# Three result buffers for a float64 decode, and scatters of token places through four disjoint views, in a fused attention and two-MoE kernel

## The chip, the cores and the metric

The kernel runs on one core of one Trainium2 chip. The metric is the device time of one execution in microseconds (us). The engines are named as in the profile: PE (TensorE's matmuls) and PEld (its weight loads), DVE (VectorE), ACT (ScalarE), POOL (GpSimd) and SP (SyncE, which here only issues DMAs). SP and POOL each send their DMAs in the order of their program: an issue that waits holds up what stands behind it.

## The reference, cut to what matters

```python
attn = linear_attention(r, k, v, w, u)             # 4 x 8 heads x 768 x 48
x = attn.transpose(0, 2, 1, 3).reshape(3072, 384)  # tokens
# first MoE: one expert of 8 for each token, d_ff 1024
expert = argmax(x @ w_gate, axis=1)
x[mask_e] = gate_w * (relu(x[mask_e] @ w1[e]) @ w2[e])
# second: one dense layer for all tokens, d_ff 2048, weights in float64
h = x @ w_in
out = ((h - tanh(h)) @ w_out).astype(float32)
```

The weights `w_in` and `w_out` come as float64 and have to be turned into float32 on the chip. A token's gated attention output goes to `xd` in DRAM, and the first MoE gathers from there the tokens of one expert at a time.

## The kernel before, in words

The program has three parts, one after the other: attention and gating (to about 184 us), the first MoE (to 415 us) and the second (to 827 us). Every fp32 matrix is split into a high and a low part (`fp32r`) and each product is made in three passes, so ACT casts the high part and DVE or POOL subtracts it from the original to get the low part.

*The first MoE* runs over 8 experts of 8 steps of 128 hidden columns: 64 steps `i`, in program order on every engine. A step issues `mm1(i+2)` (hidden layer of the step after the next: 9 matmuls into `hps`, L986; ACT's ReLU L989; DVE's low part `h`, L990), then `mm2(i)` (9 matmuls into `y`, L1011). In three steps of each expert `xg_trans` turns the next expert's gathered tokens: PE transposes into `tps` (L973), ACT casts (L974), DVE subtracts (`xt`, L975). `tps` and `hps` share four PSUM buffers.

*The weights* come by `w_load` (L76, SP) into four staging buffers `stg`, and `refill` calls `w_split` on them: ACT's cast (L84) and the subtraction (L85), one part in four by DVE and three by POOL. A staging buffer is free when its two parts are split.

*The float64 decode* fills DVE's spare time. 32 pieces of 128 x 384 numbers of the second MoE's weights are loaded by SP as 64-bit integers (`d64`, three buffers), decoded by five DVE instructions (L936 to L943) and stored by SP into `wdec` in DRAM (L951, `dec_move`), from where the second MoE's weights are loaded later. `b` lies in PSUM, `a` in one SBUF buffer, the result `f` in one of two buffers (tag `dcf`, the pool's default). `dec_move` of a step stores what the step before decoded and then issues the next piece's load. In SP's program it stands behind the step's `w_load`s.

*The places of the tokens.* For the output the kernel needs, for each place in the experts' order, the token that lies there. 24 indirect DMAs on POOL's queue (L1178), one about every two steps, scatter 128 token numbers each (`tok`) to their places (`pos`) in `permd` in DRAM; one DMA reads the whole back (`perm`, L1182) in step 54, and DVE turns it into output rows (L1186 to L1193). The places are a permutation, so no two scatters write the same element. They are written as DMAs to one tensor, and each waits until the one before it has landed.

*The overflow path* (`beyond`, L1067 to L1122) handles tokens above an expert's capacity, behind a branch on their number; it uses `permd`, the gather pool and the decode pool. In the profiled execution none of its instructions runs.

Of the kernel before, what the change touches and what calls it, by code (L numbers as in the profile page):

```python
# [8 lines left out]
F32 = mybir.dt.float32  # L9
F32R = mybir.dt.float32r  # L10
F16 = mybir.dt.float16
I32 = mybir.dt.int32
# [8 lines left out]
MIN_EXP = 2.0 ** -15 * 1.125  # L21
# [9 lines left out]
def rwkv_moe_moe_kernel(ctx: ExitStack, tc: tile.TileContext, rk_t, rkv, pk, u, wp1, wp2, out):  # L31


    nc = tc.nc
    B, C, P, _, H, D = rkv.shape
    N, DM = out.shape
# [875 lines left out]
    dcp = m1.enter_context(tc.tile_pool(name="dcp", bufs=2))  # L912
    dc, decoded = {}, []


    UNW = 384
    NU = 1536 // UNW
# [9 lines left out]
    def decode(i):  # L927

        p, q = divmod(i, NU)
        hl = dc.pop(i).bitcast(I32).rearrange("p (n t) -> p n t", t=2)  # L930
        lo, hi = hl[:, :, 0], hl[:, :, 1]

        b = psm.tile([P, UNW], I32, tag="dec", name="dec", bufs=1)
        a = dcp.tile([P, DM], I32, tag="dca", name="dca", bufs=1)[:, 0:UNW]
        f = dcp.tile([P, UNW], F32, tag="dcf", name="dcf")
        nc.vector.tensor_scalar(out=b, in0=hi, scalar1=0x07FFFFFF, scalar2=3,  # L936
                                op0=ALU.bitwise_and, op1=ALU.logical_shift_left)
        nc.vector.scalar_tensor_tensor(out=b, in0=lo, scalar=29, in1=b,
                                       op0=ALU.logical_shift_right, op1=ALU.bitwise_or)
        nc.vector.scalar_tensor_tensor(out=a, in0=hi, scalar=-0x40000000, in1=b,  # L940
                                       op0=ALU.bitwise_and, op1=ALU.bitwise_or)
        nc.vector.tensor_single_scalar(out=b, in_=hi, scalar=0x7FFFFFFF, op=ALU.bitwise_and)
        nc.vector.scalar_tensor_tensor(out=f, in0=b.bitcast(F32), scalar=MIN_EXP, in1=a.bitcast(F32),  # L943
                                       op0=ALU.is_ge, op1=ALU.mult)
        decoded.append((i, f))

# [120 lines left out]
    def beyond(q):  # L1067
# [23 lines left out]
        fetch(tk, permd, pl)  # L1091
        x = xgp.tile([P, DM], F32, tag="xg", name="ov_x")
        fetch(x, xd, tk)
        xT = dcp.tile([P, DM], F32, tag="dca", name="ov_xT", bufs=1)
        ps = psm.tile([P, CAP], F32, tag="h", name="ov_ps", bufs=4)
        for kk in range(KD):
            nc.tensor.transpose(ps[:, kk * P:(kk + 1) * P], x[:, kk * P:(kk + 1) * P], ident)
# [3 lines left out]
        for f in range(CH1):  # L1101
            if f % 2 == 0:
                wa, wb = (dcp.tile([P, DM], U64, tag="d64", name="ov_w", bufs=DB).bitcast(F32) for _ in range(2))
                fetch(wa, halves, ovr[:, f:f + 1])
                fetch(wb, halves, ovr[:, f + 1:f + 2])
            hps = psm.tile([P, CAP], F32, tag="h", name="ov_hp", bufs=4)
            for kk in range(KD):
                c0 = kk * 256 + f % 2 * P
                nc.tensor.matmul(hps[:, 0:P], lhsT=wa[:, c0:c0 + P], rhs=xT[:, kk * P:(kk + 1) * P],
                                 start=(kk == 0), stop=(kk == KD - 1))  # L1110
            h = dcp.tile([P, UNW], F32, tag="dcf", name="ov_h")
            nc.scalar.activation(out=h[:, 0:P], in_=hps[:, 0:P], func=ACTF.Relu)
            for d in range(KD):
                c0 = f % 2 * DM + d * P
                nc.tensor.matmul(yo[d][:, 0:P], lhsT=wb[:, c0:c0 + P], rhs=h[:, 0:P],
                                 start=(f == 0), stop=(f == CH1 - 1))
# [28 lines left out]
    with tc.manual_schedule():  # L1145
# [7 lines left out]
        for i in range(NC1):  # L1153
# [22 lines left out]
            for t in range(*((max(k, 0) * NT // S0) for k in (i - CH1, i - CH1 + 1))):  # L1176
                if t < NT:
                    nc.gpsimd.indirect_dma_start(  # L1178
                        out=permd, out_offset=bass.IndirectOffsetOnAxis(ap=pos[:, t:t + 1], axis=0),
                        in_=tok[:, t:t + 1], in_offset=None)  # L1180
            if i == CH1 + S0 + 2:
                nc.gpsimd.dma_start(out=perm, in_=permd.rearrange("(i p) o -> p (i o)", p=P))  # L1182
# [218 lines left out]
```

## Time and profile before

| what | value |
|---|---|
| timed runs | 825.07, 825.17, 829.99 us, median 825.17 |
| the profiled execution | 828.9 us, span 826.8 us |
| mean granted TensorE clock | 0.987 |
| PE, PEld busy | 786.1 us (95%), 702.3 us (85%) |
| DVE, ACT, POOL busy | 649.6 us (79%), 526.5 us (64%), 448.3 us (54%) |
| DMA | 89.88 MB, mean 109 GB/s |

The span is the time between the first and the last instruction in the trace, and 2.1 us of the execution lie around it. Shares of busy time are means over three parts with different limits, so the rows further below go by stretches. Idle time of an engine is put down to what ended it (`x <- y` reads: x waited for y). In the names, `hps`, `y`, `h` and `xt` are as above; `dcf` is the decode's result, `stg` a staging buffer, `ring` a buffer of split weights. DVEq, SPq and the like are an engine's sequencer or its DMA queue.

### The profile page before, as it was taken

Reading aid. Unit: us, or ns where it says so; the run is one execution under the profiler, and the core shown is the slowest. Engines: PE = TensorE matmul, PEld = TensorE weight load, DVE = VectorE, ACT = ScalarE, POOL = GpSimd, SP = SyncE. Lnnn points to the kernel's source line nnn. Section 1 sums busy time; section 2 is a strip of 40 time slices with the busy share of each in tenths; the row PEclk is TensorE's granted clock in tenths of the full one; section 3 lists DMA queues with packets and bytes.
Section 4 is the critical chain, followed back from the end, with each engine's and each line's share of the span. In section 5 each row is a group of like instructions: output and inputs, shape, how many; then the busy total and the mean of one; then the engine's idle time right before and its main releaser. Section 6 shows DMA issues by size and latency. Waiting matters only on the chain.

```text
span 826.8 us, 14401 instructions
## 1 busy us (share of the span) xinstructions
PE 786.1 (95%) x5052; PEld 702.3 (85%) x5052; DVE 649.6 (79%) x1127; ACT 526.5 (64%) x1135; POOL 448.3 (54%) x438
## 2 busy tenths in 40 slices
PE   7799999989999999997999999999999999999995
PEld 6576766789888999996989999999999999999895
DVE  6789888548888888876469888888888888888991
ACT  7778887515454444443478776776777677677870
POOL 5977876226675886656525535335344344443533
PEclk9799999999999999999999999999999999999999
DMA  8988774226688989897410000000000000000000
GB/s 202 246 222 238 220 211 129 99 71 201 201 227 236 256 224 267 258 250 177 110 56 2 1 1 39 1 1 39 1 1 29 10 1 17 23 1 0 39 1 38
DMA packets 34979, 89.88 MB, mean 109 GB/s; under 512 B 5690, under 2 KB 13022, under 8 KB 34896
## 3 DMA queue, kind: packets, MB, share of 16 engines
q1 hardware_dynamic: 30704, 78.87, 34.5%
q0 software_dynamic: 4192, 9.99, 3.9%
q8 instruction: 42, 0.69, 0.4%
q14 instruction: 41, 0.34, 0.2%
HBM read 73.10 MB, written 15.74 MB: 107 GB/s over the span
## 4 chain that ended last, share of the span: by engine, by line
PE 48%; DVE 2%; issue 1%; POOL 1%; ACT 0%; POOLq 0%; DVEq 0%; ACTq 0%
PE h L1237 23%; PE o L1285 22%; PE y L1011 2%; PE hps L986 1%; DVE t L1258 0%; DVE h L1255 0%; DVE h L1256 0%; DVE h L1254 0%; DVE t L1253 0%; POOL out_dram L1298 0%; POOL g L1274 0%; ACT g L1273 0%; POOLq L1396 0%; ACT z L1241 0%; ACT t L1243 0%
## 5 line engine op out<-in xcount | busy, mean ns | idle before, releaser
L1237 PE MATMUL h<-xb,ring 128*128 128x512 f32 x864 | 215.9, 395 | 0.7 <-DVE t L1258 0.7
L1274 POOL TENSOR_TENSOR g<-t,g 128x512 fp32r<-128x512 f32 x93 | 120.5, 1295 | 176.3 <-ACT g L1273 121.3
L1285 PE MATMUL o<-ring,g 128*128 128x384 f32 x1116 | 209.3, 336 | 0.0
L1285 PEld LDWEIGHTS o<-ring,g 128*128 128x128 f32 x1116 | 196.1, 188 | 8.1
L1237 PEld LDWEIGHTS h<-xb,ring 128*128 128x128 f32 x864 | 161.3, 188 | 31.9 <-DVE t L1258 1.1
L85 POOL TENSOR_TENSOR ring<-stg,ring 128x384 fp32r<-128x384 f32 x102 | 104.9, 1057 | 39.6 <-ACT ring L84 23.9
L1241 ACT ACTIVATE z<-h 128x512 f32<-128x512 f32 x96 | 57.5, 599 | 97.9 <-PE h L1237 97.8
L1011 PE MATMUL y<-h,ring 128*128 128x256 f32 (+7 forms) x576 | 115.5, 345 | 0.0
L986 PE MATMUL hps<-xt,ring 128*128 128x472 f32 (+6 forms) x504 | 106.8, 355 | 8.4 <-DVE xt L975 4.1
L1011 PEld LDWEIGHTS y<-h,ring 128*128 128x128 f32 x576 | 102.6, 190 | 3.5 <-DVE h L990 0.4
L986 PEld LDWEIGHTS hps<-xt,ring 128*128 128x128 f32 x504 | 90.7, 188 | 13.7 <-DVE xt L975 5.5
L1253 DVE TENSOR_TENSOR t<-t,h 128x512 f32<-128x512 f32 x96 | 65.8, 686 | 43.0 <-ACT t L1243 42.9
L84 ACT CAST ring<-stg 128x384 fp32r<-128x384 f32 x152 | 71.1, 511 | 29.3 <-DMA stg<-in_wp_dram 24.9
L1258 DVE COPY_PREDICATED t<-mk,h 128x512 f32<-128x512 uint32 x96 | 72.2, 752 | 9.9
L1255 DVE SCALAR_TENSOR_TENSOR h<-s,h 128x512 f32<-128x512 f32 x96 | 66.9, 696 | 10.0
L1245 ACT ACTIVATE s<-z,gb 128x512 f32<-128x512 f32 x96 | 69.6, 725 | 0.0
L1256 DVE SCALAR_TENSOR_TENSOR h<-z,h 128x512 f32<-128x512 f32 x96 | 66.8, 695 | 3.3
L1247 ACT ACTIVATE mk<-z,gt 128x512 f32<-128x512 f32 x96 | 69.3, 722 | 0.0
L989 ACT ACTIVATE h<-hps 128x256 fp32r<-128x256 f32 (+7 forms) x64 | 32.0, 501 | 57.7 <-PE hps L986 55.3
L1254 DVE TENSOR_TENSOR h<-h,z 128x512 f32<-128x512 f32 x96 | 66.5, 693 | 0.0
L344 ACT ACTIVATE am<-ident,dt 128x128 f32<-128x128 f32 x192 | 58.6, 389 | 7.0 <-DVE dt L337 6.9
L1273 ACT CAST g<-t 128x512 fp32r<-128x512 f32 x93 | 57.6, 619 | 8.0 <-DVE t L1258 5.8
(233 smaller groups left out, 1116.2 us busy)
## 6 DMA issues: line engine op xcount, KB each, us to landing
stg<-in_wp_dram SPq DMA_DIRECT2D x64, 384.0 KB
n<-in_rkv_dram SPq DMA_DIRECT2D x24, 576.0 KB
d<-in_wp_dram SPq DMA_DIRECT2D x32, 384.0 KB
t<-in_rk_t_dram SPq DMA_DIRECT2D x48, 192.0 KB
wdec<-dcf SPq DMA_DIRECT2D x32, 192.0 KB
xd<-xs SPq DMA_DIRECT2D x24, 192.0 KB
stg<-wdec SPq DMA_DIRECT2D x12, 384.0 KB
wl<-wdec SPq DMA_DIRECT2D x2, 768.0 KB
```

The source lines that it names most:

```text
L84: nc.scalar.copy(out=dst[:, 0, sl], in_=of)
L85: eng.tensor_tensor(out=dst[:, 1, sl], in0=of, in1=dst[:, 0, sl].bitcast(F32), op=ALU.subtract)
L986: nc.tensor.matmul(ps, lhsT=wf(a, kk), rhs=xt[e][b][:, kk, :], start=(n == 0), stop=(n == 8))
L1011: nc.tensor.matmul(yps[d], lhsT=wf(a)[:, d * P:(d + 1) * P], rhs=h2[:, b, :], start=(f == 0 and n == 0), stop=(f == CH1 - 1 and n == 2))
L1237: nc.tensor.matmul(ps, lhsT=wf(a, kk), rhs=xb[j][:, b, kk, :], start=(n == 0), stop=(n == 8))
L1245: nc.scalar.activation(out=s, in_=z, func=ACTF.Square, scale=G_K ** 0.5, bias=gb)
L1247: nc.scalar.activation(out=mk, in_=z, func=ACTF.Relu, scale=-1.0, bias=gt2)
L1255: nc.vector.scalar_tensor_tensor(out=ps, in0=s, scalar=G_K * G_D, in1=ps, op0=ALU.add, op1=ALU.mult)
L1256: nc.vector.scalar_tensor_tensor(out=ps, in0=z, scalar=G_A, in1=ps, op0=ALU.subtract, op1=ALU.mult)
L1258: nc.vector.copy_predicated(out=t, mask=mk.bitcast(U32), data=ps)
L1274: nc.gpsimd.tensor_tensor(out=g[:, 1, :], in0=ww, in1=g[:, 0, :].bitcast(F32), op=ALU.subtract)
L1285: nc.tensor.matmul(ops[q], lhsT=gg[i][:, b, q * P:(q + 1) * P], rhs=wf(a), start=(f == 0 and n == 0), stop=(f == CH2 - 1 and n == 2))
```

## The change

The result `f` has three buffers, and the decode's intermediate `a` is the same memory as `f`, read as integers: the third instruction (L940, now L942) writes it and the fifth (L943, now L945) multiplies it in place. The buffer of `a` goes; the overflow path, which used its tag for `xT`, takes a gather buffer. `permd` is seen through four views that the program takes for disjoint; scatter `t` goes through view `t % 4`. Line numbers behind L914 rise by two.

```diff
--- before.py
+++ after.py
@@ -912,6 +912,8 @@
     dcp = m1.enter_context(tc.tile_pool(name="dcp", bufs=2))
     dc, decoded = {}, []
 
+    permv = dram_disjoint_views(permd, 4)
+
 
     UNW = 384
     NU = 1536 // UNW
@@ -931,8 +933,8 @@
         lo, hi = hl[:, :, 0], hl[:, :, 1]
 
         b = psm.tile([P, UNW], I32, tag="dec", name="dec", bufs=1)
-        a = dcp.tile([P, DM], I32, tag="dca", name="dca", bufs=1)[:, 0:UNW]
-        f = dcp.tile([P, UNW], F32, tag="dcf", name="dcf")
+        f = dcp.tile([P, UNW], F32, tag="dcf", name="dcf", bufs=3)
+        a = f.bitcast(I32)
         nc.vector.tensor_scalar(out=b, in0=hi, scalar1=0x07FFFFFF, scalar2=3,
                                 op0=ALU.bitwise_and, op1=ALU.logical_shift_left)
         nc.vector.scalar_tensor_tensor(out=b, in0=lo, scalar=29, in1=b,
@@ -940,7 +942,7 @@
         nc.vector.scalar_tensor_tensor(out=a, in0=hi, scalar=-0x40000000, in1=b,
                                        op0=ALU.bitwise_and, op1=ALU.bitwise_or)
         nc.vector.tensor_single_scalar(out=b, in_=hi, scalar=0x7FFFFFFF, op=ALU.bitwise_and)
-        nc.vector.scalar_tensor_tensor(out=f, in0=b.bitcast(F32), scalar=MIN_EXP, in1=a.bitcast(F32),
+        nc.vector.scalar_tensor_tensor(out=f, in0=b.bitcast(F32), scalar=MIN_EXP, in1=f,
                                        op0=ALU.is_ge, op1=ALU.mult)
         decoded.append((i, f))
 
@@ -1091,7 +1093,7 @@
         fetch(tk, permd, pl)
         x = xgp.tile([P, DM], F32, tag="xg", name="ov_x")
         fetch(x, xd, tk)
-        xT = dcp.tile([P, DM], F32, tag="dca", name="ov_xT", bufs=1)
+        xT = xgp.tile([P, DM], F32, tag="xg", name="ov_xT")
         ps = psm.tile([P, CAP], F32, tag="h", name="ov_ps", bufs=4)
         for kk in range(KD):
             nc.tensor.transpose(ps[:, kk * P:(kk + 1) * P], x[:, kk * P:(kk + 1) * P], ident)
@@ -1108,7 +1110,7 @@
                 c0 = kk * 256 + f % 2 * P
                 nc.tensor.matmul(hps[:, 0:P], lhsT=wa[:, c0:c0 + P], rhs=xT[:, kk * P:(kk + 1) * P],
                                  start=(kk == 0), stop=(kk == KD - 1))
-            h = dcp.tile([P, UNW], F32, tag="dcf", name="ov_h")
+            h = dcp.tile([P, UNW], F32, tag="dcf", name="ov_h", bufs=3)
             nc.scalar.activation(out=h[:, 0:P], in_=hps[:, 0:P], func=ACTF.Relu)
             for d in range(KD):
                 c0 = f % 2 * DM + d * P
@@ -1176,7 +1178,7 @@
             for t in range(*((max(k, 0) * NT // S0) for k in (i - CH1, i - CH1 + 1))):
                 if t < NT:
                     nc.gpsimd.indirect_dma_start(
-                        out=permd, out_offset=bass.IndirectOffsetOnAxis(ap=pos[:, t:t + 1], axis=0),
+                        out=permv[t % 4], out_offset=bass.IndirectOffsetOnAxis(ap=pos[:, t:t + 1], axis=0),
                         in_=tok[:, t:t + 1], in_offset=None)
             if i == CH1 + S0 + 2:
                 nc.gpsimd.dma_start(out=perm, in_=permd.rearrange("(i p) o -> p (i o)", p=P))
```

All engines issue the same instructions in the same order as before; what they wait for differs. The first place is DVE at two decodes in the first MoE, around 240 to 247 us of the trace, before and after. `dec`, `dca` and `dcf` are `b`, `a` and `f`; in brackets are the semaphores that a row waits for, DMAHW ones for SP's transfers.

```order
L940 SCALAR_TENSOR_TENSOR dca<-d_4769,dec 128x384 [waits DVE_49]
L942 TENSOR_SCALAR dec<-d_4769 128x384 [waits DVE_49]
L943 SCALAR_TENSOR_TENSOR dcf<-dec,dca 128x384 [waits DMAHW3_49,DVE_49]
L85 TENSOR_TENSOR ring_4168<-stg,ring_4168 128x384 [waits DMAHW2_49,Activation_49]
L990 SCALAR_TENSOR_TENSOR h_4935<-hps,h_4935 128x440 [waits Activation_49]
L936 TENSOR_SCALAR dec<-d_4820 128x384 [waits DMAHW4_49,DVE_49]
L938 SCALAR_TENSOR_TENSOR dec<-d_4820,dec 128x384 [waits DVE_49]
L940 SCALAR_TENSOR_TENSOR dca<-d_4820,dec 128x384 [waits DVE_49]
L942 TENSOR_SCALAR dec<-d_4820 128x384 [waits DVE_49]
L943 SCALAR_TENSOR_TENSOR dcf<-dec,dca 128x384 [waits DMAHW6_49,DVE_49]
```

The same place in the changed program:

```order
L942 SCALAR_TENSOR_TENSOR dcf<-d_4768,dec 128x384 [waits DMAHW0_49,DVE_49]
L944 TENSOR_SCALAR dec<-d_4768 128x384 [waits DVE_49]
L945 SCALAR_TENSOR_TENSOR dcf<-dec,dcf 128x384 [waits DVE_49]
L85 TENSOR_TENSOR ring_4168<-stg,ring_4168 128x384 [waits DMAHW2_49,Activation_49]
L992 SCALAR_TENSOR_TENSOR h_4931<-hps,h_4931 128x440 [waits Activation_49]
L938 TENSOR_SCALAR dec<-d_4818 128x384 [waits DMAHW4_49,DVE_49]
L940 SCALAR_TENSOR_TENSOR dec<-d_4818,dec 128x384 [waits DVE_49]
L942 SCALAR_TENSOR_TENSOR dcf<-d_4818,dec 128x384 [waits DMAHW3_49,DVE_49]
L944 TENSOR_SCALAR dec<-d_4818 128x384 [waits DVE_49]
L945 SCALAR_TENSOR_TENSOR dcf<-dec,dcf 128x384 [waits DVE_49]
```

The wait for a store of an older result (DMAHW3, DMAHW6) has gone from the decode's fifth instruction to the third instruction of the decode behind it: the store of DMAHW3 was waited for in the first decode shown, and now is in the second.

The second place is POOL between two gathers, late in the first MoE; the DMASW semaphores are those of POOL's own transfers.

```order
L1178 DMA permd<-tok,pos 3072x1 [waits DMASW4_49]
L85 TENSOR_TENSOR ring_72<-stg,ring_72 128x384 [waits DMAHW2_49,Activation_49]
L1178 DMA permd<-tok,pos 3072x1 [waits DMASW5_49]
L85 TENSOR_TENSOR ring_72<-stg,ring_72 128x384 [waits DMAHW5_49,PE_49,Activation_49]
L85 TENSOR_TENSOR ring_72<-stg,ring_72 128x384 [waits PE_49,Activation_49]
L85 TENSOR_TENSOR ring_4167<-stg,ring_4167 128x384 [waits DMAHW0_49,Activation_49]
L85 TENSOR_TENSOR ring_4167<-stg,ring_4167 128x384 [waits DMAHW1_49,PE_49,Activation_49]
L1178 DMA permd<-tok,pos 3072x1 [waits DMASW6_49]
```

The same eight rows in the changed program:

```order
L1180 DMA permd<-tok,pos 3072x1 [waits DMASW6_49]
L85 TENSOR_TENSOR ring_72<-stg,ring_72 128x384 [waits DMAHW2_49,Activation_49]
L1180 DMA permd<-tok,pos 3072x1 [waits DMASW7_49]
L85 TENSOR_TENSOR ring_72<-stg,ring_72 128x384 [waits DMAHW5_49,PE_49,Activation_49]
L85 TENSOR_TENSOR ring_72<-stg,ring_72 128x384 [waits PE_49,Activation_49]
L85 TENSOR_TENSOR ring_4167<-stg,ring_4167 128x384 [waits DMAHW0_49,Activation_49]
L85 TENSOR_TENSOR ring_4167<-stg,ring_4167 128x384 [waits DMAHW1_49,PE_49,Activation_49]
L1180 DMA permd<-tok,pos 3072x1 [waits DMASW0_49]
```

Of the scatters, the first waited for the one just ahead (on DMASW4), the second for the first one (DMASW5), the third for the second (DMASW6); now each waits for the one four before it.

## Rows read from the trace of the kernel before

**Rows 1.** Windows: stretch, length, each engine's busy us (count), TensorE clock, DMA share, GB/s.
```profile
...
236.00:298.00 62.00, 61.43 (x317) 57.35 (x316) 52.75 (x89) 30.78 (x67) 45.13 (x45) 1.00 0.90 256
...
357.00:391.00 34.00, 28.86 (x155) 27.57 (x154) 24.27 (x43) 13.70 (x32) 24.34 (x25) 0.95 0.85 208
...
415.00:827.00 412.00, 402.00 (x2019) 362.39 (x2017) 331.70 (x487) 289.08 (x522) 174.90 (x143) 1.00 0.03 13
...
```

**Rows 2.** Waits of PE, 184 to 415: total us, times, longest.
```profile
...
PE hps L986 <- DVE xt L975: 4.1, 4, 2.8
PE hps L986 <- DVE h L990: 3.4, 3, 1.9
...
```

**Rows 3.** Timeline of PE: start, us, operation, idle time before it.
```profile
...
202.98 0.70 PE L986 MATMUL hps<-xt,ring 128*128 128x472 f32 x2 [0.63 <-DVE xt L975]
...
374.11 1.85 PE L986 MATMUL hps<-xt,ring 128*128 128x384 f32 x9 [1.95 <-DVE h L990]
375.80 1.74 PE L1011 MATMUL y<-h,ring 128*128 128x384 f32 x9
...
381.41 1.46 PE L986 MATMUL hps<-xt,ring 128*128 128x376 f32 x7 [0.37 <-DVE xt L975]
385.66 0.70 PE L986 MATMUL hps<-xt,ring 128*128 128x376 f32 x2 [2.79 <-DVE xt L975]
386.16 3.08 PE L1011 MATMUL y<-h,ring 128*128 128x384 f32 x9
...
```

**Rows 4.** Windows of PE alone, around its longest stall: PEclk, DMA share, GB/s.
```profile
...
386.20:389.20 3.00, 3.00 (x11) 0.50 0.81 20
...
```

**Rows 5.** Waits of all engines over the span: total us, times, longest.
```profile
...
POOL permd L1178 <- DMA permd<-tok,pos: 25.9, 10, 4.3
ACT ring L84 <- DMA stg<-in_wp_dram: 24.9, 15, 5.7
...
DVE dcf L943 <- DMA wdec<-dcf: 16.4, 12, 2.7
...
```

**Rows 6.** Timeline of DVE, 346 to 395.
```profile
...
357.46 0.56 DVE L943 SCALAR_TENSOR_TENSOR dcf<-dec,dca 128x384 f32<-128x384 f32 x1 [1.17 <-DMA wdec<-dcf]
...
367.70 0.56 DVE L943 SCALAR_TENSOR_TENSOR dcf<-dec,dca 128x384 f32<-128x384 f32 x1 [2.74 <-DMA wdec<-dcf]
...
371.20 0.55 DVE L940 SCALAR_TENSOR_TENSOR dca<-d,dec 128x384 int32<-128x384 int32 x1
...
380.34 0.56 DVE L943 SCALAR_TENSOR_TENSOR dcf<-dec,dca 128x384 f32<-128x384 f32 x1 [1.66 <-DMA wdec<-dcf]
...
385.07 0.54 DVE L975 TENSOR_TENSOR xt<-tps,xt 128x376 fp32r<-128x376 f32 x1
...
```

**Rows 7.** Timeline of SP's DMA issues: start, us, queue, line, transfer.
```profile
...
363.13 0.34 SPq L76 DMA_DIRECT2D stg<-in_wp_dram  x1
363.56 0.39 SPq L951 DMA_DIRECT2D wdec<-dcf  x1
...
```

**Rows 8.** Waits of SP's queue, 215 to 395.
```profile
...
SPq L76 <- POOL ring L85: 60.4, 25, 8.1
...
```

**Rows 9.** Timeline of POOL at one scatter.
```profile
...
356.07 0.99 POOL L1178 DMA_INDIRECT permd<-tok,pos  x1 [4.32 <-DMA permd<-tok,pos]
...
```

**Rows 10.** Instructions on tile permd: ns min/median/max, first and last start; then landing.
```profile
...
L1178 POOL DMA_INDIRECT permd<-tok,pos x24: 990/1004/1142, 217.8 to 382.1; - x24
...
DMA to landing us min/median/max: 2.4/4.3/6.6
...
```

**Rows 11.** Instructions of L85, 215 to 392: ns min/median/max, first and last start.
```profile
...
L85 DVE TENSOR_TENSOR ring<-stg,ring x25: 542/549/2935, 221.0 to 387.4; 128x384 fp32r<-128x384 f32 x25
...
```

**Rows 12.** Groups of DVE by line, 215 to 392: count, busy us, mean ns, idle.
```profile
...
L85 DVE TENSOR_TENSOR ring<-stg,ring 128x384 fp32r<-128x384 f32 x25 | 23.3, 932 | 0.0
...
```

**Rows 13.** Timelines of DVE and of POOL at one split that was blocked.
```profile
...
253.19 2.94 DVE L85 TENSOR_TENSOR ring<-stg,ring 128x384 fp32r<-128x384 f32 x1
...
253.72 1.98 POOL L85 TENSOR_TENSOR ring<-stg,ring 128x384 fp32r<-128x384 f32 x2
...
```

## The prediction

> **What bounds the kernel now.** I read the windows first, one row per stretch of the program [rows 1]. The second MoE (415 to 827 us) keeps TensorE's matmuls busy 402 of 412 us, moves almost nothing by DMA and contains no edited line, so nothing can be won there; whatever the first MoE gives up ahead of it is passed on to the end whole. The first MoE's stretches differ: 61.4 of 62 us busy from 236 to 298, but only 28.9 of 34 us from 357 to 391, at a granted clock of 0.95. The reader is to see that the loss is in this last stretch.
>
> The waits of TensorE from 184 to 415 us come next [rows 2]: 4.1 us on VectorE's `xt` (the low half of the transposed tokens), 3.4 us on VectorE's `h`. Of the 4.1 us, 0.63 us falls at 202.98 [rows 3], before the first decode result is asked for, so 6.9 us of stalls (4.1 + 3.4 - 0.63) lie where the decode runs. The timeline shows the largest: 1.95 us at 374.11, 0.37 at 381.41 and 2.79 at 385.66 [rows 3]. The stall of 2.79 us costs more than itself: the nine `y` matmuls at 386.16 take 3.08 us where the same nine at 375.80 take 1.74 [rows 3], and the granted clock from 386.2 to 389.2 is 0.50 of full speed, so the lower level, 1.2 GHz, after that idle time [rows 4]. That is 1.34 us more. Altogether 6.9 + 1.34 = 8.2 us hang on a late VectorE.
>
> Why VectorE is late stands in the waits of all engines [rows 5]: its decode's last instruction (L943) waits 16.4 us in 12 waits for the DMA that stores an earlier result, because `dcf` has two buffers. Its timeline shows the worst place [rows 6]: L943 waits 1.17 us at 357.46, 2.74 at 367.70 and 1.66 at 380.34, and a decode later stands the `xt` at 385.07 for which TensorE has been waiting.
>
> Why the store is late is read on SyncE's queue [rows 7]: the result finished at 357.46 + 0.56 = 358.0 us is not sent before 363.56, because the queue works in order and the weight load ahead of it (L76) leaves at 363.13. Such loads wait 60.4 us in 25 waits for GpSimd's split to free a staging buffer [rows 8]. And GpSimd itself waits 25.9 us in 10 waits, up to 4.3 us, for the scatter of tokens before the present one [rows 5]; one of 4.32 us ends at 356.07 [rows 9], just ahead of that blocked load. So the two edits sit on one chain: scatter, split, staging buffer, load, store, decode, `xt` and `h`, TensorE.
>
> **The change part by part.** The programs of all engines issue the same instructions in the same order; semaphores and buffers differ. So nothing is added to any queue, and the terms are waits alone.
>
> *Scatters through four views.* A scatter now waits for the one four before it. 24 scatters stand between 217.8 and 382.1 us, so about 7.1 us apart (164.3/23), and the fourth before is some 28 us old, while the longest landing is 6.6 us [rows 10]. I take all 25.9 us as gone from GpSimd, bounds 0 and 25.9. What it gains directly on the path is nothing, since TensorE never waits for GpSimd here [rows 2]; the gain is that splits run earlier and SyncE's queue clears. What is late next on GpSimd is ScalarE's cast of the weights, for which its splits wait already.
>
> *Three result buffers, the intermediate in place.* The wait for a store moves from the fifth instruction of the next decode but one to the third instruction of the decode after that. Cost of moving it forward: two decode instructions of 0.56 us that are now queued behind the wait, with `h`, `xt` and the split behind them as before. Gain: one decode period. At the worst place the store that ended its wait at 367.70 would be asked for by the third instruction of the next decode, at 371.20 [rows 6]; if that decode comes 2.74 us earlier because the wait is gone, 368.46 is still after the landing. I take 14 to 16.4 of the 16.4 us as gone, bounds 0 (each wait comes back one decode later) and 16.4. The three waits quoted are 5.6 us; the `xt` at 385.07 could then start by 379.5, and TensorE, without its own 1.95 and 0.37 us of stall, asks for it at about 381.41 + 1.46 - 2.32 = 380.6. So the stalls go with some 1.1 us to spare. That is little, so I don't take the whole 8.2 us.
>
> *`xT` in the gather pool, `h` of the overflow path.* These lie in a branch that this input doesn't take in the trace. Zero, both ways; the memory is the same, since one 384-column buffer goes and one comes.
>
> *The sum.* Between 0 and 8.2 us (below nothing only by the port, below), with 7.0 taken, near the upper end, since the stall rows name this chain; 1.2 us is left for new short waits. From the profiled execution, 828.9 us (span 826.8): 828.9 - 7.0 = 821.9. The three timed runs are 825.07, 825.17 and 829.99, so the profiled one lies 3.7 us above their median. If that distance is stalls of this kind, which come and go (the difference between the runs, 4.9 us, is close to the stalls of 0.37 + 2.79 and the 1.34 of low clock), the changed kernel ends near 821.9; if profiling adds it everywhere, near 825.17 - 7.0 = 818.2. I weigh the first three to one: 821.0 us.
>
> **A price of its own: the port between VectorE and GpSimd.** VectorE's splits (L85) take 0.55 us at the median and 2.94 at most, 0.93 on average over 25 [rows 11, 12]; the one of 2.94 us runs beside two GpSimd splits of together 1.98 us [rows 13]. Its extra is thus 25 x (0.93 - 0.55) = 9.6 us already. When GpSimd no longer pauses for scatters, its splits stand closer together, and this can grow.
>
> The Trainium skill, "SBUF — State Buffer", section "Who interferes with whom", says that a VectorE instruction with two SBUF inputs and a GpSimd instruction that reads SBUF exclude each other for a whole instruction; that speaks against this change. By that rule one split would lose at most one GpSimd instruction. The trace agrees with the blocking, but its 2.94 us outlasts both GpSimd splits rather than one, and the measurement decides.
>
> **The rivals.**
> 1. *The stalls move on rather than go.* ScalarE waits 24.9 us for weight loads [rows 5], and DMA engines are busy 0.85 to 0.90 [rows 1]; if loads land no earlier although issued earlier, ScalarE's casts hold up its ReLU, then `h`, then TensorE. Then I take a third of the 8.2 us, 2.7 us: 826.2 from the profile, 822.5 from the median, weighed as above 825.3. For it: the stage's DMA share. Against it: 236 to 298 us runs at the highest share, 0.90 and 256 GB/s, with 0.57 us of stall in 62, and 357 to 391 moves 208 GB/s x 34 us = 7.1 MB, which in 34 - 7 = 27 us is 262 GB/s, hardly more.
> 2. *All goes, and is judged from the median.* 825.17 - 8.2 = 817.0, give or take a us. For it: every stall named in rows 2 is on VectorE. Against: the spare time of 1.1 us.
> 3. *Slower, by GpSimd's splits in unbroken rows.* Place: VectorE's splits, each blocked by a run of GpSimd splits. Price: 25 times the longest against the mean, 25 x (2.94 - 0.93) = 50 us of VectorE. It decides from a mean of 0.93 + 16.4/25 = 1.59 us on; at a mean of 2.2 it takes 31.8 us against 16.4 saved, 15.4 us net, some 12 of them on TensorE: 840.9 from the profile, 837.2 from the median, weighed 840. For it: the split in rows 13. Against it: gathers and scatters stay between GpSimd's splits.
> 4. *What is saved is used up on VectorE.* If each of the 25 splits is held up by one whole GpSimd split, it takes 0.55 + 1.98/2 = 1.54 us, 25 x (1.54 - 0.93) = 15.3 us more than now against 16.4 saved; or the stores are waited for as long as now, one instruction group later. Either way no gain: 825.2. For it: the split in rows 13, which alone lost 2.4 us. Against it: the median split, 0.55 us, is as long as a decode instruction of the same size, so more than half aren't held up at all, and the waits that the program lists are for older transfers.
>
> **How the numbers follow.** Forecast 0.60 (by itself 818 to 824.5 us, eight times in ten), rival 1 0.20, rival 2 0.10, rival 3 0.05, rival 4 0.05. About 1%, 8 us, is what a measurement tells from no change; the bound for faster is 816.9. Half of rival 2 and a twelfth of the forecast lie below it: 0.05 + 0.05 = 0.10. Rival 3 is the chance of slower, 0.05, and the rest, 0.85, is within 1%. The range from 816.0 to 826.5 us holds forecast, rivals 1 and 4 and most of rival 2, so some nine in ten by these chances; I keep it that wide because the relation of profile and median is open.
>
> **What would show it.** Right: the wait for the earlier scatter gone from GpSimd's waits; the decode's wait for its store under 2 us in all; TensorE's stalls on `xt` and `h` between 236 and 391 us under 1.5 us, no stretch at half clock there, and the second MoE's first matmul some 7 us earlier than now. Wrong in the size: ScalarE's waits for weight loads grow and TensorE still waits for `h`. Wrong in the sign: VectorE's splits average over 1.6 us. A second MoE of another length than 412 us would speak against the whole reading.

## The result, and the profile after

| | before | changed |
|---|---|---|
| timed, six runs each on one chip, median | 825.75 us (825.07 to 829.99) | 816.25 us (815.03 to 819.61) |
| ratio of the two | | 0.9881, 95% interval 0.9857 to 0.9905 |
| profiled execution, its span | 828.9, 826.8 us | 815.03, 812.9 us |
| first MoE, from its first hidden matmul to the second MoE's first | 184.31 to 415.29: 231.0 us | 179.83 to 401.38: 221.6 us |
| second MoE, to the end of the span | 411.5 us | 411.5 us |

The change is faster by 9.5 us at the medians, 1.2%, where 4.2 us were forecast (825.17 to 821.0). A second comparison, with 10 and 31 runs, gave 0.9943 (0.9926 to 0.9960), 816.92 against 822.14 us, so 5.2 us: the changed kernel takes the same time in both to 0.7 us, the kernel before doesn't. The two profiled executions lie further apart than the medians, 13.9 us: that of the changed kernel is the fastest of its six runs, and 4.5 us of the distance lie ahead of the first MoE, where no line was edited.

The windows of the changed kernel (stretch, length, busy us and count of each engine, granted clock, DMA share, GB/s) stand against [rows 1]. The stretch from 350 to 377 us does the work of 357 to 391 before, up to the branch.

```profile
...
232.00:294.00 62.00, 62.00 (x321) 58.04 (x320) 52.33 (x92) 30.60 (x66) 45.53 (x46) 1.00 0.96 265
350.00:377.00 27.00, 26.69 (x156) 26.28 (x155) 24.49 (x41) 13.63 (x31) 19.54 (x20) 1.00 0.89 250
401.00:813.00 412.00, 402.09 (x2020) 362.47 (x2018) 331.50 (x487) 289.15 (x522) 174.85 (x143) 0.99 0.03 14
...
```

TensorE is busy 26.7 of 27 us there, at full clock, where it was busy 28.9 of 34. The stretch moves 250 GB/s against 208: nearly the same bytes (6.8 against 7.1 MB) in less time. TensorE's waits (total us, times, longest) answer to [rows 2], and its timeline (start, us, operation, idle time before) to [rows 3].

```profile
...
PE hps L988 <- DVE xt L977: 0.9, 2, 0.6
PE hps L988 <- ACTq L1127: 0.9, 1, 0.9
...
```

```profile
...
179.83 3.49 PE L988 MATMUL hps<-ring,ring 128*128 128x256 f32 x27 [0.59 <-DVE ring L584]
...
198.49 0.69 PE L988 MATMUL hps<-xt,ring 128*128 128x472 f32 x2 [0.63 <-DVE xt L977]
...
371.62 1.36 PE L988 MATMUL hps<-xt,ring 128*128 128x376 f32 x7
373.28 0.61 PE L988 MATMUL hps<-xt,ring 128*128 128x376 f32 x2 [0.31 <-DVE xt L977]
373.74 1.74 PE L1013 MATMUL y<-h,ring 128*128 128x384 f32 x9
...
401.38 6.46 PE L1239 MATMUL h<-xb,ring 128*128 128x512 f32 x27
...
```

Only the stall at the first expert change (198.49, before any decode) and 0.31 us at 373.28 are left of 7.5 us on `xt` and `h`; the nine `y` matmuls behind the latter take 1.74 us, not 3.08, at full granted clock. The first and the last row are the ends of the first MoE in the table. GpSimd's and VectorE's waits from 200 to 392 us answer to [rows 5]:

```profile
...
POOL ring L85 <- ACT ring L84: 39.6, 24, 3.1
...
POOL permd L1180 <- issue: 3.1, 19, 0.2
...
```

```profile
...
DVE h L992 <- ACT h L991: 16.5, 15, 3.7
...
DVE dec L938 <- DMA d<-in_wp_dram: 1.5, 3, 0.8
...
```

The 25.9 us for the earlier scatter and the 16.4 us for stores are gone. Other waits grew: GpSimd's for ScalarE's casts to 39.6 us, from 20.3 before in the same window, and VectorE's for the ReLU to 16.5 us, from 9.2. TensorE's waits above show nothing of either. SyncE's queue [rows 8] and VectorE's splits [rows 12] didn't change so plainly. Here are the waits of SyncE's queue from 200 to 385 us, and the group of VectorE's splits (count, busy us, mean ns, idle) from 200 to 392:

```profile
...
SPq L76 <- POOL ring L85: 65.4, 34, 7.6
...
```

```profile
...
L85 DVE TENSOR_TENSOR ring<-stg,ring 128x384 fp32r<-128x384 f32 x29 | 24.8, 855 | 3.0 <-ACT ring L84 3.0
...
```

Weight loads still wait 65.4 us for GpSimd's splits; from 200 to 392 us, the same window for both kernels, it is 76.8 us against 67.1 before. The queue did not clear. The splits average 855 ns; taken over this same window the first profile of before has 891. Last, the scatters [rows 10]:

```profile
...
L1180 POOL DMA_INDIRECT permd<-tok,pos x24: 989/1004/1367, 213.2 to 368.3; - x24
...
DMA to landing us min/median/max: 2.2/6.1/9.1
...
```

They land later than before (6.1 us at the median, up to 9.1) and nothing waits for them for long: only VectorE's use of the whole list does, behind the stage's last scatter.

### The profile page after: what moved, and what is told of

It reads as the page before. It is cut to its first block, busy times and chain, and to the rows that moved or that the text cites. A ratio compares the mean times of both kernels' runs of the same rounds, so it can differ in the third digit from the quotient of the medians.

```text
span 812.9 us, 14403 instructions
## 1 busy us (share of the span) xinstructions
PE 780.9 (96%) x5052; PEld 699.3 (86%) x5052; DVE 648.6 (80%) x1127; ACT 526.0 (65%) x1135; POOL 450.7 (55%) x438
## 4 chain that ended last, share of the span: by engine, by line
PE 49%; DVE 2%; issue 1%; POOL 1%; ACT 0%; POOLq 0%; DVEq 0%; ACTq 0%
PE h L1239 24%; PE o L1287 22%; PE y L1013 2%; PE hps L988 1%; DVE t L1260 0%; DVE h L1257 0%; DVE h L1258 0%; DVE h L1256 0%; DVE t L1255 0%; POOL out_dram L1300 0%; POOL g L1276 0%; ACT g L1275 0%; POOLq L1398 0%; ACT z L1243 0%; ACT t L1245 0%
## 5 line engine op out<-in xcount | busy, mean ns | idle before, releaser
L85 POOL TENSOR_TENSOR ring<-stg,ring 128x384 fp32r<-128x384 f32 x102 | 105.0, 1052 | 57.1 <-ACT ring L84 50.2
L84 ACT CAST ring<-stg 128x384 fp32r<-128x384 f32 x152 | 70.8, 512 | 19.1 <-DMA stg<-in_wp_dram 18.6
```

What stands on the lines that cost most here:

```text
L84: nc.scalar.copy(out=dst[:, 0, sl], in_=of)
L85: eng.tensor_tensor(out=dst[:, 1, sl], in0=of, in1=dst[:, 0, sl].bitcast(F32), op=ALU.subtract)
```

## The experiments

The first question is which edit does it, and by which way. Theory A: TensorE loses what VectorE waits for stores, and the third buffer ends that alone. Theory B: the late scatter is the root. "First MoE" is always the length as in the table above, from one profiled execution.

**Buffers alone.** Everything changed but the scatters.

```diff
-                        out=permv[t % 4], out_offset=...
+                        out=permd, out_offset=...
```

> Three buffers and the intermediate in place, scatters as before. Theory A (TensorE loses only what VectorE waits for stores of results; the third buffer ends that by itself): no wait of the decode for its store, first MoE (from its first hidden matmul to the second MoE's first) 221.5 to 223 us against 231.0 before and 221.6 with both edits, ratio 0.988 to 0.991; GpSimd still waits some 25 us for its scatters, at no cost. Theory B (the late scatter is the root: it holds the split, the staging buffer, the load and the store behind it, so with it the stores are late by more than a decode period): over 4 us of waits for the store stay, ScalarE still waits 25 us for weight loads, first MoE 226 us or more, ratio 0.993 or more.

Measured: ratio 0.9975 (0.9949 to 1.0001), first MoE 228.5 us. The waits for stores are gone, as A said, and yet only 2.5 of the 9.4 us came; against two later profiles of before (further down) it is 0.7 and 0.1 us, and the interval of the ratio includes 1. The rows of this kernel: VectorE's waits, GpSimd's waits, VectorE's splits.

```profile
...
DVE dec L938 <- DMA d<-in_wp_dram: 4.9, 5, 1.5
...
```

```profile
...
POOL permd L1180 <- DMA permd<-tok,pos: 24.0, 10, 3.5
...
```

```profile
...
L85 DVE TENSOR_TENSOR ring<-stg,ring 128x384 fp32r<-128x384 f32 x29 | 35.1, 1210 | 1.1 <-ACT ring L84 1.1
...
```

No wait on a store is left; VectorE waits 4.9 us for pieces to decode. GpSimd still waits 24.0 us for scatters, and VectorE's splits, the same number as in the changed kernel, take 35.1 us instead of 24.8. One of them is worth a look: GpSimd, VectorE and TensorE around 380 us in the same kernel.

```profile
...
378.95 0.99 POOL L1180 DMA_INDIRECT permd<-tok,pos  x1 [3.50 <-DMA permd<-tok,pos]
379.97 4.86 POOL L85 TENSOR_TENSOR ring<-stg,ring 128x384 fp32r<-128x384 f32 x5
...
```

```profile
...
379.96 5.30 DVE L85 TENSOR_TENSOR ring<-stg,ring 128x384 fp32r<-128x384 f32 x1
385.18 1.00 DVE L992 SCALAR_TENSOR_TENSOR h<-hps,h 128x384 fp32r<-128x384 f32 x2
...
```

```profile
...
385.78 1.66 PE L1013 MATMUL y<-h,ring 128*128 128x384 f32 x8 [1.77 <-DVE h L992]
...
```

A scatter waits 3.50 us for the one before. Five splits for which everything lay ready have queued up behind it, and GpSimd works them off in one row, 4.86 us. VectorE's own split starts beside the first of them and ends 0.4 us behind the last: 5.30 us for an operation of 0.55. `h` stands behind it, at 385.18, and TensorE waits 1.77 us for `h`. That is a way from the scatter to TensorE that has no store in it. Theory A falls as worded, since the third buffer alone doesn't bring the gain. B's length and ratio came, but not its way: it put what is left on stores that stay late, and none does.

**Views alone.** The kernel before with the four views.

```diff
+    permv = dram_disjoint_views(permd, 4)
...
-                        out=permd, out_offset=...
+                        out=permv[t % 4], out_offset=...
```

> Scatters through four views alone; two buffers and an intermediate of its own, as before. Theory A: GpSimd's 25.9 us of waits go, but the decode's waits for its store stay at 10 us or more, since the store stands behind weight loads that wait for splits anyway; first MoE 227 to 231 us, ratio 0.995 to 1.0. Theory B: the waits for the store fall to 5 us or less, first MoE 224 us or less, ratio 0.992 or less.

Measured: 0.9934 (0.9910 to 0.9959), first MoE 222.9 us. Here is VectorE's wait for stores:

```profile
...
DVE dcf L944 <- DMA wdec<-dcf: 8.6, 7, 2.6
...
```

It is 8.6 us, between the two expectations, as the ratio is, and nearly the whole gain is there all the same (8.1 of 9.4 us; in time, 0.9934 can't be told from the 0.9943 of both edits). VectorE's splits take 25.0 us. So half of the waits for stores cost TensorE almost nothing here. The kernel before, profiled again further down, also waits 8.6 us for its stores, and takes 229.2 us: among VectorE's losses the two differ in the splits, 33.8 against 25.0 us, and hardly in the rest. So in these profiles the views don't work by bringing the stores forward.

**Both edits with two buffers.**

```diff
-        f = dcp.tile([P, UNW], F32, tag="dcf", name="dcf", bufs=3)
+        f = dcp.tile([P, UNW], F32, tag="dcf", name="dcf", bufs=2)
...
-            h = dcp.tile([P, UNW], F32, tag="dcf", name="ov_h", bufs=3)
+            h = dcp.tile([P, UNW], F32, tag="dcf", name="ov_h", bufs=2)
```

> Both edits, but two result buffers instead of three, with the intermediate in place, so that the wait for a store comes two instructions earlier than before the change. Theory A: the decode waits 16 us or more (some 1.2 us more for each wait, up to 30 us), first MoE 229 to 236 us, ratio 0.997 to 1.007. Theory B: with the scatters out of the way the stores are early, 8 us of waits or less, first MoE 225 us or less, ratio 0.993 or less.

Measured: 0.9975 (0.9956 to 0.9993), first MoE 227.8 us, 13.0 us of waits for stores, in six waits of up to 3.8 us. With the scatters out of the way the wait two instructions earlier costs 4.4 us more of waiting than with views alone, and TensorE 4.9 us (timed on one chip, 822.81 against 818.13 us). It is neither theory's length. The form in place needs its third buffer; since the waits for stores of one and the same kernel vary as much (further down), how much of this the two instructions make is not shown.

**Stores ahead of weight loads.** The kernel before, with another order on SyncE.

```diff
+            dec_move()
             while freed:
                 w_load(*freed.pop(0))
-            dec_move()
```

> The kernel before, with one exchange on SyncE: a step's store of the decoded result and the next piece's load go ahead of the step's weight loads instead of behind them. If the store was late because it stood behind weight loads that wait for staging buffers: the decode's waits fall from 16.4 us to 5 us or less with two buffers, first MoE 223 to 226 us, ratio 0.989 to 0.994; weight loads come later by at most the store's issue. If the store was late because the transfer itself takes long: waits stay above 10 us, first MoE 229 to 231, ratio 0.998 to 1.002.

Measured: 0.9912 (0.9878 to 0.9945), first MoE 222.3 us, a little below the 223 expected, no wait for a store in the decode and none for a piece, whose loads move with the stores. So the prediction's reading of SyncE's queue [rows 7] holds: the stores were late because they stood behind weight loads. GpSimd's waits and VectorE's splits in this kernel:

```profile
...
POOL permd L1178 <- DMA permd<-tok,pos: 17.9, 10, 4.7
...
```

```profile
...
L85 DVE TENSOR_TENSOR ring<-stg,ring 128x384 fp32r<-128x384 f32 x29 | 31.5, 1086 | 2.6 <-ACT ring L84 2.3 <-issue 0.2
...
```

The scatters still make GpSimd wait 17.9 us and VectorE's splits take 31.5 us, and TensorE hardly loses by it. The row of five GpSimd splits comes here too (4.88 us from 378.87 on). VectorE and TensorE around it:

```profile
...
378.27 0.55 DVE L990 SCALAR_TENSOR_TENSOR h<-hps,h 128x376 fp32r<-128x376 f32 x1 [0.29 <-issue]
378.74 5.43 DVE L85 TENSOR_TENSOR ring<-stg,ring 128x384 fp32r<-128x384 f32 x1
...
```

```profile
...
380.69 1.72 PE L1011 MATMUL y<-h,ring 128*128 128x384 f32 x9
...
```

It holds a VectorE split for 5.43 us, but the `h` that TensorE needs next has run ahead of that split, and the nine `y` matmuls go through without a stall. With buffers alone VectorE was one split further back in its program, and the same row caught it ahead of `h`. So in this pair the row costs TensorE something only where VectorE is late already.

**What buffers alone leave.** Two kernels from "buffers alone" ask whether it is the port (theory P) or the waits for pieces (theory D). In the first, SyncE loads the next piece ahead of the step's weight loads:

```diff
+            for k, _ in decoded:
+                if k + DB < ND:
+                    dec_load(k + DB)
             while freed:
                 w_load(*freed.pop(0))
             dec_move()
...
-            if i + DB < ND:
-                dec_load(i + DB)
```

> Three buffers with scatters as before, and on SyncE the loads of the next pieces to decode ahead of the step's weight loads (stores stay behind them). Theory P (what buffers alone leave is VectorE's split held up by rows of GpSimd splits that follow a late scatter): the waits for pieces go, the splits still average about 1.2 us, first MoE 226 to 229 us against 228.5 with buffers alone. Theory D (it is the waits for pieces, 4.9 us, that stood behind the same weight loads): first MoE 224 us or less, with VectorE's splits still at 1.2 us.

Measured: 0.9986 (0.9950 to 1.0023), first MoE 229.1 us in the profile, no wait for a piece any more, and VectorE's splits:

```profile
...
L85 DVE TENSOR_TENSOR ring<-stg,ring 128x384 fp32r<-128x384 f32 x28 | 42.0, 1501 | 0.6 <-ACT ring L84 0.6
...
```

They grew to 42.0 us. In this execution the 4.9 us went and nothing was won, which speaks for P and against D. But of the nine timed runs behind the ratio four took 815.3 to 817.1 us, no more than with both edits, and five, the profiled one among them, 821.3 to 825.5. What differs between these executions isn't on record, so D is not excluded. In the second kernel GpSimd does all splits:

```diff
-                w_split(p, part, eng=nc.gpsimd if part else nc.vector)
+                w_split(p, part, eng=nc.gpsimd)
```

> Three buffers with scatters as before, and all four parts of each weight split on GpSimd, none on VectorE. Theory P: VectorE is rid of some 35 us of splits and TensorE's stalls on it fall below 1.5 us, first MoE 224 us or less, unless GpSimd, with some 25 splits of 1.0 us more, becomes late itself: then ScalarE's waits for weight loads grow beyond 27 us and TensorE waits for split weights. Theory D: TensorE's stalls go down by at most the time that the splits took themselves, 25 x 0.55 us spread over the stage, waits for pieces stay at 4 us or more, first MoE 225 to 228 us.

Measured: first MoE 223.4 us in the profile, where P said 224 or less and D 225 to 228, but only 0.9974 (0.9945 to 1.0003) timed, 820.16 against 822.14 us, where both edits gave 816.92 on that chip. VectorE's waits there:

```profile
...
DVE h L992 <- ACT h L991: 27.8, 20, 3.5
DVE dec L938 <- DMA d<-in_wp_dram: 14.8, 8, 3.1
...
```

With no split of its own VectorE waits 14.8 us for pieces, and TensorE's stalls on it are 2.3 us (1.3, 0.8 and 0.2), above the 1.5 that P expected, against 6.6 with buffers alone. ScalarE's waits for weight loads (26.1 us, 26.8 with buffers alone) are as long as ever, so in the profile they are not what costs TensorE. The profile supports P, though the edit takes the splits' own time from VectorE too, not only what they wait. The timed runs say that the arrangement as a whole buys little; the profiled execution, 818.79 us, is the second fastest of its ten, and why profile and timing part here stays open.

**Both edits and stores first.**

```diff
+            dec_move()
             while freed:
                 w_load(*freed.pop(0))
-            dec_move()
```

> Both edits, and stores and piece loads ahead of the weight loads on SyncE. Whatever the theory, TensorE has 1.8 us of stalls left in this stage, 0.9 of them at the branch: first MoE 220.5 to 222 us against 221.6 with both edits, time within 0.3% of theirs. A clear gain beyond that would say that weight loads or stores still cost something that the waits don't list.

Measured: 0.9941 (0.9922 to 0.9961), first MoE 222.0 us: the same as both edits. Nothing more was won by this order.

**The changed kernel again.**

> The changed kernel once more, profiled anew. The first MoE takes 221 to 223 us again and the second 411.5; its first hidden matmul of the first MoE lies anywhere from 179 to 185 us, as the attention part differs from execution to execution. Were the profiled execution of before slow inside the first MoE only by chance, this one would differ from 221.6 by several us.

Measured: 0.9943 (0.9926 to 0.9960), first MoE 221.2 us, its start at 183.96 us. So the first MoE repeats to 0.4 us, and the part before it, which no edit touches, moves by 4.1 us between two executions.

**The kernel before again, twice, and two views.**

> The kernel before, profiled anew, on a chip where its median may differ from 825. Its first MoE takes 226 to 232 us again (231.0 in the first profile) while the second takes 411.5; GpSimd waits 20 us or more for scatters and the decode 10 us or more for its stores. If the first MoE comes out near 222, the loss of the first profile was chance and most of the change's gain with it.

> The kernel before a third time, for the spread of its first MoE: 226 to 232 us, with the difference to the first and second profile in TensorE's stalls on VectorE's xt and h. If the spread is below 1 us, what differs between executions of before lies in the attention part alone.

Measured: first MoE 229.2 and 228.6 us, so 2.4 us below the first profile at most; TensorE's stalls on VectorE 6.3 and 6.9 us. The ratios, 0.9991 (0.9963 to 1.0018) and 1.0000 (0.9983 to 1.0017), say how far the comparison can be trusted. Two expectations were missed, 10 us or more for the stores (8.6 and 6.2) and, in the first of the two, 20 us or more for scatters (16.2; 23.1 in the second). Here are VectorE's waits for stores and its splits in the first of the two:

```profile
...
DVE dcf L943 <- DMA wdec<-dcf: 8.6, 7, 2.5
...
```

```profile
...
L85 DVE TENSOR_TENSOR ring<-stg,ring 128x384 fp32r<-128x384 f32 x29 | 33.8, 1164 | 0.0
...
```

What VectorE loses is put together differently from execution to execution: 8.6 us for stores and 33.8 us in splits here, 16.4 and 24.9 in the first profile.

```diff
-    permv = dram_disjoint_views(permd, 4)
+    permv = dram_disjoint_views(permd, 2)
...
-                        out=permv[t % 4], out_offset=...
+                        out=permv[t % 2], out_offset=...
```

> The changed kernel with two views instead of four, so that a scatter waits for the one two before it. The longest landing seen with four views was 9.1 us and scatters are some 7 us apart, so two before is 14 us old: waits for scatters stay under 2 us, first MoE 221 to 223 us, time within 0.3% of the changed kernel's. If it is over 225 us, more than two scatters are in flight at a time and four are needed.

Measured: 0.9945 (0.9925 to 0.9965), first MoE 221.5 us. GpSimd's wait for scatters:

```profile
...
POOL permd L1180 <- DMA permd<-tok,pos: 0.8, 1, 0.8
...
```

Two in flight are enough.

**All profiles side by side.** The three ways in which VectorE loses time in this stage, each as the wait or line group of 200 to 392 us gives it, in us, and TensorE's stalls on VectorE's `xt`, `h` and decode. The splits stand with their own time, some 16 us (28 to 30 of 0.55 us).

| kernel | waits for stores | waits for pieces | its splits | sum | TensorE's stalls | first MoE |
|---|---|---|---|---|---|---|
| before, three profiles | 16.4 / 8.6 / 6.2 | 1.4 / 0.4 / 0.6 | 24.9 / 33.8 / 33.6 | 42.7 / 42.8 / 40.4 | 7.5 / 6.3 / 6.9 | 231.0 / 229.2 / 228.6 |
| pieces first, three buffers | 0 | 0 | 42.0 | 42.0 | 6.6 | 229.1 |
| both edits, two buffers | 13.0 | 0 | 27.9 | 40.9 | 4.4 | 227.8 |
| buffers alone | 0 | 4.9 | 35.1 | 40.0 | 6.6 | 228.5 |
| views alone | 8.6 | 1.0 | 25.0 | 34.6 | 1.7 | 222.9 |
| stores first, before | 0 | 0 | 31.5 | 31.5 | 1.4 | 222.3 |
| both edits, two profiles | 0 / 0 | 1.5 / 1.5 | 24.8 / 23.6 | 26.3 / 25.1 | 0.9 / 0.6 | 221.6 / 221.2 |
| both, two views | 0 | 1.8 | 24.4 | 26.2 | 0.6 | 221.5 |
| both, stores first | 0 | 0 | 24.7 | 24.7 | 1.0 | 222.0 |
| no splits, three buffers | 0 | 14.8 | 0 | 14.8 | 2.3 | 223.4 |

The stalls give the length: the first MoE less its stalls is 220.6 to 221.9 us in nine of the thirteen profiles. In the other four (the first two of before, pieces first, and both edits with two buffers) it is 222.5 to 223.5, and these are the four in which the granted clock falls to 0.50 behind a stall.

What makes the stalls is less sharp. Up to a sum of some 35 us the first MoE takes 221 to 223 us, whatever the sum is made of; from 40 us on it takes 228 to 231. That reads as if VectorE had so much slack beside its own work, and only what goes beyond it reached TensorE. It is a pattern found in these profiles, and no run tests it: nothing lies between 34.6 and 40.0, and where in the stage a loss falls must matter too. VectorE's time to spare, its wait for the ReLU, is 8.1 us with stores first (222.3 us) and 11.1 us with buffers alone (228.5 us). The last row doesn't lie on this line: there GpSimd has VectorE's splits to do as well.

## Why the prediction was wrong

**What bounds the kernel** was right. The whole gain that belongs to the change lies in the first MoE, 9.4 us, and the second takes 411.5 us in both profiles. The stalls named in [rows 2 to 4] are the ones that went, with the half clock behind the longest, and the signs named for being right came: no wait for scatters or stores, 0.31 us of stalls where 1.5 were allowed, no stretch at half clock; the second MoE's first matmul came 13.9 us earlier where some 7 were expected. What failed is the size: 4.2 us were forecast and 9.5 measured. Of the 5.3 us between them the choice of the base made 2.8 (821.0 - 818.2) and the sum 2.4 (9.4 - 7.0).

**The sum was too small**, the smaller of the two steps that failed: of at most 8.2 us, 7.0 were taken, and 9.4 came. The stalls gave 6.6 us (7.5 less 0.9) and the half clock 1.34, so the part that was held back, 1.2 us, was held back wrongly. Another 1.5 us (9.4 - 6.6 - 1.34) stands in no wait row. Part of it is that a stall costs more than its row gives: from 381.41 to the next start at 385.66 [rows 3] pass 4.25 us, of which seven matmuls without a stall take 1.22 (1.57/9 each, from the changed kernel's step from 375.31 to 376.88), so 3.03 us are lost for a wait of 2.79. Other stalls do the same. Here are the ends of one stretch of matmuls before, and of the same stretch in the changed kernel with the step used above:

```profile
...
366.29 1.74 PE L1011 MATMUL y<-h,ring 128*128 128x384 f32 x9
...
390.76 1.74 PE L1011 MATMUL y<-h,ring 128*128 128x384 f32 x9
...
```

```profile
...
359.58 1.74 PE L1013 MATMUL y<-h,ring 128*128 128x384 f32 x9
...
375.31 1.72 PE L988 MATMUL hps<-xt,ring 128*128 128x376 f32 x9
376.88 1.73 PE L1013 MATMUL y<-h,ring 128*128 128x384 f32 x9
...
```

From 366.29 to 390.76 pass 24.47 us, from 359.58 to 376.88 only 17.30. Of the 7.17 us the rows of stalls give 4.80 (1.95 + 0.37 + 2.79 - 0.31) and the half clock 1.34, so 1.03 us of the 1.5 are time around stalls that no row lists. The reason for holding back was a spare time of 1.1 us at the `xt`; in the changed kernel that `xt` costs 0.31 us.

**From the profile to the median** the larger error was made, the weighing of three to one. The 3.7 us by which the profiled execution of before lay above its median were put down three to one to stalls of this kind. The changed kernel's profile reaches the first MoE 4.5 us earlier (179.83 against 184.31), before any edited line has run, and its second profile at 183.96 again. The three profiles of before start it at 184.31, 181.01 and 182.39. So the attention part alone moves by as much as the distance in question, while the first MoE of before moves by 2.4 us; how the 3.7 us divide isn't on record, since only a profiled execution shows its stages. With the median as the base, 825.17 - 9.4 = 815.8, close to the 816.25 measured. In the later comparisons the two profiled executions of before are the slowest of their ten runs, 2.5 and 2.7 us above the median, and the timed gain (4.7 to 5.2 us) is smaller than the profiled one of the first MoE (7.1 to 8.0 us, against 221.2 to 221.5). That this gain is near the 4.2 us forecast is luck, since the profiled stage gains more than the 7.0 us taken there too. Why the profiled executions of before come out slow wasn't tried.

**Scatters through views.** That no wait for scatters would be left was right. That they gain "directly on the path nothing" and only by clearing SyncE's queue was wrong twice: the queue's waits for splits stayed (60.4 before, 65.4 us after), and with the buffers in place but not the views 6.9 us of the 9.4 were still missing. Their way to TensorE is also the row of GpSimd splits after a late scatter, and VectorE's split beside it; one such stall, of 1.77 us, was followed through above.

**Three buffers.** The waits for stores went entirely, at the upper end. By themselves they are worth 0.1 to 2.5 us, by which profile of before is taken, and 1.3 on top of the views (222.9 to 221.6), too little for the timed runs to tell. The prediction took one term for a chain of both edits; it should have asked what each leaves.

**The rivals.** Rival 3 had the right place, VectorE's splits beside GpSimd's, and the wrong sign: it feared rows of splits when GpSimd no longer pauses. Rows form behind pauses, where splits that have become ready queue up; in the changed kernel the three splits behind a scatter and three gathers still make one. With the views VectorE's splits average 814 to 962 ns in six profiles, without them 891 to 1501 in six. The 891 is the first profile of before, whose splits take as long in all as the changed kernel's (24.9 and 24.8 us): in the pair that the prediction is about, what VectorE got rid of is the 16.4 us of waits for stores, as the prediction had it, and only against the later profiles of before is it mostly the splits. Rival 1 fell: ScalarE's waits for weight loads went from 24.9 to 18.6 us. Rival 2 had the nearest number, 817.0, by taking the median as its base and the whole of the stalls. Rival 4 fell for both edits, but with buffers alone what it feared is there: against the first profile of before the 16.4 us for stores go, while the splits take 10.2 us more and the waits for pieces 3.5 more.

## What to carry to other kernels

Look at an engine's losses of different kinds (waits for a buffer, for a load, for another engine) together, and at the stalls that they make on the engine that bounds the stage. Here one kind taken away could be replaced by others with nothing won (buffers alone), and half of a kind could stay at hardly any cost (views alone); an edit that wins nothing doesn't show that what it took away was harmless. A wait on a queue does more than delay what stands behind it: what has become ready in the meantime then runs in one row, and here a VectorE split beside such a row stood still until its end. Indirect writes to one DRAM tensor that are known to be disjoint should be told so; two views were enough here. And a profiled execution is one execution: here the median of the runs was the better base for the forecast, and the kernel with the stalls had to be profiled more than once.

## What the runs showed of the hardware that was not expected

A VectorE split of 0.55 us with both inputs in SBUF, started beside a row of five GpSimd splits (4.86 us), took 5.30 us: it waits for the whole row and not for one instruction of it. In other kernels it took 5.43 us (stores first) and 5.46 us (before again) beside rows of 4.88 and 4.87 us. The same happened beside three, 3.41 us beside 2.98 in the changed kernel:

```profile
...
349.69 3.41 DVE L85 TENSOR_TENSOR ring<-stg,ring 128x384 fp32r<-128x384 f32 x1
...
```

```profile
...
349.69 2.98 POOL L85 TENSOR_TENSOR ring<-stg,ring 128x384 fp32r<-128x384 f32 x3
...
```

The granted clock fell to half after the idle time of 2.79 us [rows 4] and did not in the changed kernel after 0.31 us. The length of one idle time doesn't decide it alone: with both edits and two buffers the clock fell to 0.50 after 1.90 us, and in the third profile of before it stayed at 1.00 after 2.30 us. And the kernel before took 825.8 and 825.2 us in two comparisons and 822.1 in two others, while the changed kernel took 816.3 us where before took 825.8, and 816.9 where it took 822.1: the kernel with the stalls is the one that varied.
